# Squared-ReLU attention and a two-layer block on one core: quad 5 turned by a transposing transfer

## The chip, the cores and the metric

The kernel runs on one core of one Trainium2 chip. The metric is the device time of one execution in microseconds (us), the median of three runs. A core has five engines with a queue of instructions each: TensorE (PE in the profile; its weight loads are PEld), VectorE (DVE), ScalarE (ACT), GpSimd (POOL) and SyncE (SP). Transfers run on 16 DMA engines that the queues share.

## The reference

Attention with a squared ReLU in place of softmax, for 8 batch rows, 12 heads, 448 positions and a head size of 64. Its result, as 3584 rows of 768, goes through two matrix products with a PReLU between them.

```python
scores = scale * np.matmul(q, k.transpose(0, 1, 3, 2))      # scale = 1/sqrt(64)
attn = np.maximum(scores, 0.0) ** 2 / S                     # S = 448
attn_out = np.matmul(attn, v)                               # (8, 12, 448, 64)
x = attn_out.transpose(0, 2, 1, 3).reshape(B * S, H * D)    # (3584, 768)
h = x @ w_in                                                # w_in (768, 2048)
g = np.maximum(h, 0.0) + alpha * np.minimum(h, 0.0)
out = g @ w_out                                             # w_out (2048, 768)
```

All inputs and the output are float32.

## The kernel before

The work is written out in the order in which each engine does it. Four heads of one batch row are a *quad*: there are 24, three for each batch row (0 to 2 belong to row 0, 3 to 5 to row 1, 6 to 8 to row 2). For each quad:

- q and k are loaded and cast to bf16 by GpSimd's queue (`load_qk`), v likewise (`load_v`);
- q and k are turned, so that the head size lies on the partitions (the tile `T`). This happens in one of two ways: 28 small transposes on TensorE and two copies out of PSUM (`turn_pe`, quads 0 to 5), or two copies into a tile `perm` on VectorE and one transposing transfer on SyncE's queue (`turn_dma`, quads 6 and later);
- seven chunks of scores go through ReLU (`sc`) and square (`sq`), and the product with v sums over the seven chunks (`attnv`); two copies, half each on ScalarE and VectorE, leave it in `xT`.

For each batch row `f1(b, ff)` makes block `ff` of 16 of the first product and its PReLU, which goes into `gT`; `f2(sb, c, hf)` makes 128 output rows of one half of w_out's columns from all 16 blocks of `gT`, for two batch rows at a time. A burst of attention work for the next rows stands between these long products.

```python
    raw_pool = ctx.enter_context(tc.tile_pool(name="raw", bufs=3))
    v_pool = ctx.enter_context(tc.tile_pool(name="v", bufs=7))
    perm_pool = ctx.enter_context(tc.tile_pool(name="perm", bufs=2))
    T_pool = ctx.enter_context(tc.tile_pool(name="T", bufs=4))
    # ... cut ...
    def hold():                       # the PSUM bank taken longest ago, kept until take() gives it back
        i = min(range(8), key=lambda i: (taken[i], i))
        taken[i] = 10**9
        return i
    # ... cut ...
    def load_w_out(h):
        nc.gpsimd.dma_start(out=w_out_sb[:, h], in_=w_out_v[h])
    # ... cut ...
    def turn_pe(n, parts=(("q", 0, NJ, "D"), ("k", 0, NJ, "D"))):
        if n not in T:
            T[n] = T_pool.tile([128, 2, NJ, 128], BF16, tag="T", name="T")
        for name, lo, hi, eng in parts:
            ps = take_bank().bitcast(BF16)
            for j in range(lo, hi):
                for s in range(2):
                    nc.tensor.transpose(ps[64 * s:64 * s + 64, 128 * j:128 * j + 128], raw[(n, name)][:, s, j], ident)
            dst = T[n][:, "qk".index(name), lo:hi].rearrange("p j c -> p (j c)")
            copy = nc.vector.tensor_copy if eng == "D" else nc.scalar.copy
            copy(dst, ps[:, 128 * lo:128 * hi])

    def turn_dma(n):
        p = perm_pool.tile([128, 2, NJ, 2, D], BF16, tag="perm", name="perm")
        for i, name in enumerate("qk"):
            nc.vector.tensor_copy(p[:, i], raw.pop((n, name)).rearrange("p s j d -> p j s d"))
        t = T_pool.tile([128, 2, NJ, 128], BF16, tag="T", name="T")
        nc.sync.dma_start_transpose(out=t.rearrange("p a j c -> p (a j) c"),
                                    in_=p.rearrange("p a j s d -> p (a j s d)"))
        T[n] = t
    # ... cut ...
    def f1_out(ps, b, ff):            # PReLU of one block, then one waiting square
        neg = neg_pool.tile([128, S], F32, tag="neg", name="neg")
        nc.scalar.activation(neg, ps, ACTF.Relu, scale=-1.0)
        nc.vector.scalar_tensor_tensor(gT[b // 2][:, ff, (b % 2) * S:(b % 2) * S + S],
                                       neg, beta_sb[:, ff:ff + 1], ps, ALU.mult, ALU.add)
        sq(1)
    # ... cut ...
    f1s(0, 10, 12)
    sc(ch(3, 6, 7) + ch(4, 0, 2, "AA"))
    f1s(0, 12, 16)
    f2(0, 0, 0)
    sc(ch(4, 2, 5, "AAADAAA"))
    attnv(3)
    sc(ch(4, 5, 7, "AAAAAAD"))
    turn_pe(5)
    sq(3)
    sq(2, "A")
    load_qk(8)
    load_v(8)
    f2(0, 1, 0)
    sc(ch(5, 0, 3))
    attnv(4)
    sc(ch(5, 3, 5, "AAAADAA"))
    sq(3)
    sq(2, "A")
    f2(0, 2, 0)
    sc(ch(5, 5, 7, "AAAAAAD"))
    sq(1, "A")
    sq(1)
    # ... cut ...
    early = []
    for ff in range(4):
        ps = take_bank()[:, :S]
        f1_mm(ps, 1, ff, range(4))    # four of six matmuls: those of quads 3 and 4
        early.append(ps)
        if ff == 1:
            attnv(5)
    for ff in range(KF):
        if ff < 4:
            f1_mm(early[ff], 1, ff, range(4, KM))
            f1_out(early[ff], 1, ff)
        else:
            f1(1, ff)
        if ff in (1, 4, 7):
            turn_dma(6 + ff // 3)
        if ff == 11:
            load(9)
            load(10)
    f2(0, 3, 0)
    run(some(3))                      # the first scores of quad 6
    f2(0, 3, 1)
    # ... cut ...
```

The letters in `ch(...)` say which engine does the ReLU of a chunk: A for ScalarE, D for VectorE.

Of the kernel before, what the change touches and what calls it, by code (L numbers as in the profile page):

```python
# [11 lines left out]
BF16 = mybir.dt.bfloat16  # L12
# [8 lines left out]
def kernel(  # L21
# [10 lines left out]
    nc = tc.nc  # L32
    B, H, S, D = q.shape
# [3 lines left out]
    KM = d_model // 128  # L37
    KF = d_ff // 128
# [5 lines left out]
    singles = ctx.enter_context(tc.tile_pool(name="singles", bufs=1))  # L44
# [14 lines left out]
    w_out_sb = singles.tile([128, 2, KF, HALF], BF16)  # L59
    alpha_sb = singles.tile([128, KF], F32)  # L60
    beta_sb = singles.tile([128, KF], F32)
    psum = ps_pool.tile([128, 8, 512], F32)


# [3 lines left out]
    def take(lo, n):  # L68
        clock[0] += 1
        for i in range(lo, lo + n):  # L70
            taken[i] = clock[0]

    def take_pair():
        lo = min((0, 2, 4, 6), key=lambda i: (max(taken[i], taken[i + 1]), i))
        take(lo, 2)
        return psum[:, lo:lo + 2]

    def hold():
# [5 lines that stand above are left out]
    def take_bank():  # L84
        i = min(range(8), key=lambda i: (taken[i], i))
        take(i, 1)
        return psum[:, i]
# [4 lines left out]
    def load_qk(n):  # L92
        b, g = divmod(n, NG)
        for name, src in (("q", q), ("k", k)):
            t = raw_pool.tile([128, 2, NJ, D], BF16, tag=name, name=f"{name}raw")
            flat = src[b].rearrange("(m two) (pp j) d -> (two pp) m (j d)", two=2, j=NJ)
            nc.gpsimd.dma_start(out=t.rearrange("p m j d -> p m (j d)"), in_=flat[:, 2 * g:2 * g + 2])  # L97
            raw[(n, name)] = t

    def load_v(n):  # L100
        b, g = divmod(n, NG)
        t = v_pool.tile([128, 2, NJ, D], BF16, tag="v", name="vraw")
        flat = v[b].rearrange("(m two) (pp j) d -> (two pp) m (j d)", two=2, j=NJ)
        nc.gpsimd.dma_start(out=t.rearrange("p m j d -> p m (j d)"), in_=flat[:, 2 * g:2 * g + 2])  # L104
        vraw[n] = t

    w_in_v = moe_w_in.rearrange("(g hf e pp) f -> hf e pp g f", hf=2, e=2, pp=64)
    w_out_v = moe_w_out.rearrange("(kf p) (h c) -> h p kf c", p=128, h=2)
# [5 lines left out]
                nc.gpsimd.dma_start(out=w_in_sb[64 * hf:64 * hf + 64, :, e, lo:hi],  # L114
                                    in_=w_in_v[hf, e, :, :, lo:hi])

    def load_w_out(h):
        nc.gpsimd.dma_start(out=w_out_sb[:, h], in_=w_out_v[h])

    FIRST = 4  # L120
    first, flat0 = {}, {}
    for name, src, eng, hi in (("q", q, nc.sync, NJ), ("k", k, nc.scalar, FIRST)):
# [7 lines left out]
                        in_=flat0["k"][:, :, FIRST * D:])  # L130
# [12 lines left out]
    T = {}  # L143
# [21 lines that stand above are left out]
# [31 lines left out]
    def attnv(n):  # L196
        ps = take_pair()
        vv = vraw.pop(n)
        for j in range(NJ):
            a = att.pop((n, j))  # L200
            for r in range(2):
                for s in range(2):
                    nc.tensor.matmul(ps[64 * s:64 * s + 64, r, :S],  # L203
                                     vv[64 * r:64 * r + 64, s, j, :],
                                     a[64 * r:64 * r + 64, s],
                                     start=(j == 0), stop=(j == NJ - 1))
        b, g = divmod(n, NG)
        if g == 0:
            xT[b] = xT_pool.tile([128, NG, 2, S], BF16, tag="xT", name="xT")
        if n == 0:  # L210
            nc.scalar.activation(xT[b][:, g], ps[:, :, :S], ACTF.Copy, scale=out_scale)
            return
        nc.scalar.activation(xT[b][:, g, 0], ps[:, 0, :S], ACTF.Copy, scale=out_scale)  # L213
        nc.vector.tensor_scalar(xT[b][:, g, 1], ps[:, 1, :S], out_scale, None, ALU.mult)  # L214

    late = []

    def sc(chunks):

        for n, j, eng in chunks:  # L220
            late.append((n, j, relu(score_mm(n, j), eng)))

    def sq(k=99, eng="D"):
        for g in late[:k]:
            square(*g, eng)
        del late[:k]
# [8 lines left out]
    def f1_mm(ps, b, ff, ks):  # L235
        for km in ks:
            nc.tensor.matmul(ps, w_in_sb[:, km // 2, km % 2, bass.ts(ff, 128)],  # L237
                             xT[b][:, km // 2, km % 2, :],
                             start=(km == 0), stop=(km == KM - 1))

    def f1_out(ps, b, ff):
        if b // 2 not in gT:
            gT[b // 2] = g_pool.tile([128, KF, 2 * S], BF16, tag="g", name="gT")
# [5 lines that stand above are left out]
# [6 lines left out]
    def f2(sb, c, hf, parts=((0, HALF),)):  # L255
        o = o_pool.tile([128, HALF], F32, tag="o", name="osb")
        for lo, hi in parts:
            ps = take_bank()[:, :hi - lo]
            for ff in range(KF):
                nc.tensor.matmul(ps, gT[sb][:, ff, bass.ts(c, 128)], w_out_sb[:, hf, ff, lo:hi],  # L260
                                 start=(ff == 0), stop=(ff == KF - 1))
            nc.scalar.copy(o[:, lo:hi], ps)  # L262
            for u in range(2):
                blk = 2 * c + u
                b, j = 2 * sb + blk // NJ, blk % NJ
                rows = out[b * S:(b + 1) * S].rearrange("(pp j) d -> j pp d", j=NJ)
                eng = nc.scalar if u and hi - lo < HALF else nc.sync
                eng.dma_start(out=rows[j][:, hf * HALF + lo:hf * HALF + hi], in_=o[64 * u:64 * u + 64, lo:hi])  # L268
# [4 lines left out]
    def ch(n, lo, hi, p=pat):  # L273
        return [(n, j, p[j]) for j in range(lo, hi)]
# [22 lines left out]
    sq(1)  # L297
    sc([(1, 4, "D"), (1, 5, "A"), (1, 6, "A")])
    sq(2)
    load_w_out(0)  # L300
    load_v(3)
    early = {}
    todo = []
# [8 lines left out]
    sc(ch(2, 0, 3, "AAA"))  # L312
    sq(3)
    attnv(1)
    load_qk(5)
    load_v(4)
    load_v(5)
    load_w_out(1)
    todo = [(ff, km) for ff in range(4) for km in range(4)]
    sc(ch(2, 3, 5, "AAAAAAA"))  # L320
    sq(2)
# [14 lines left out]
    def f1s(b, lo, hi):  # L336
        for ff in range(lo, hi):
            f1(b, ff)
# [9 lines left out]
        load(n + 2)  # L348

    turn_pe(3)  # L350
    load_qk(6)
    load_v(6)
    f1s(0, 4, 6)
    sc(ch(3, 0, 3))
    f1s(0, 6, 8)
# [2 lines left out]
    ps = take_bank()[:, :S]  # L358
    f1_mm(ps, 0, 9, range(KM))
    turn_pe(4, (("q", 0, NJ, "A"), ("k", 0, NJ, "D")))  # L360
    f1_out(ps, 0, 9)
    load_qk(7)
    load_v(7)
    f1s(0, 10, 12)
    sc(ch(3, 6, 7) + ch(4, 0, 2, "AA"))
    f1s(0, 12, 16)
    f2(0, 0, 0)
    sc(ch(4, 2, 5, "AAADAAA"))
    attnv(3)
    sc(ch(4, 5, 7, "AAAAAAD"))  # L370
    turn_pe(5)
    sq(3)
    sq(2, "A")
    load_qk(8)
    load_v(8)
    f2(0, 1, 0)
    sc(ch(5, 0, 3))
    attnv(4)
    sc(ch(5, 3, 5, "AAAADAA"))
    sq(3)  # L380
    sq(2, "A")
    f2(0, 2, 0)
    sc(ch(5, 5, 7, "AAAAAAD"))
    sq(1, "A")
    sq(1)


    chunks = [(n, j) for n in range(2 * NG, NQ) for j in range(NJ)]
# [12 lines left out]
        sq()  # L401

    early = []
    for ff in range(4):
        ps = take_bank()[:, :S]
        f1_mm(ps, 1, ff, range(4))
        early.append(ps)
        if ff == 1:
            attnv(5)
    for ff in range(KF):  # L410
        if ff < 4:
            f1_mm(early[ff], 1, ff, range(4, KM))
            f1_out(early[ff], 1, ff)
        else:
            f1(1, ff)
        if ff in (1, 4, 7):
# [4 lines that stand above are left out]
# [77 lines left out]
```

## Time and profile before

| what | value |
|---|---|
| time, median of 3 runs | 387.88 us (387.86 to 388.0) |
| span of the profiled execution | 386.1 us |
| transposes on TensorE (L152) | 2 x 84, from quads 0 to 5 |
| transposing transfers (T<-perm) | 18 |
| loads by GpSimd's queue (software_dynamic) | 22.45 MB |
| outputs and transposing transfers (mostly hardware_dynamic) | 19.65 MB |

In a row of the profile, a line such as L260 is the line of the kernel, "x16" the number of instructions, and `out<-in` what is written from what. The chain of waits is followed back from the last instruction, at each step to what released it; its pieces are given in order of time as start, length, what. A wait in square brackets is the idle time of an engine before a group and what ended it. The rows with 40 digits or numbers cut the span into 40 slices of 9.65 us: the digits are busy shares in tenths. The lines named most often are L174 (scores), L203 (the product with v), L237 (first product), L260 (second product), L152 (transposes on TensorE), L160 (copies into perm), L162 (the transposing transfer), L246 (gT).

### The profile page before, as it was taken

The numbers are of one execution on the slowest core, as the hardware profiler recorded it, in microseconds if no ns is written. First come the engines' busy times: TensorE is split into PE (matmuls) and PEld (weight loads), VectorE is DVE, ScalarE is ACT, GpSimd is POOL, SyncE is SP. The second block draws the span as 40 slices with busy tenths as digits, with TensorE's granted clock in tenths as the row PEclk, the third lists the DMA queues.
The fourth block names the chain that finished last, engine by engine and source line by source line (L and its number), as shares of the span: only waits on it lengthen the run. The fifth ranks groups of instructions, "written<-read, shape, count | busy, mean of one in ns | idle before, by whom it ended". The sixth has DMA issues, their size and how long they took to land.

```text
span 386.1 us, 7917 instructions
## 1 busy us (share of the span) xinstructions
PE 377.9 (98%) x3228; PEld 211.1 (55%) x3228; DVE 265.8 (69%) x421; ACT 206.2 (53%) x332; POOL 64.0 (17%) x95
## 2 busy tenths in 40 slices
PE   7799999999999999999999999999999999999996
PEld 6444564555665456555555455654555545655564
DVE  4987786776868978789655896689754887626300
ACT  5978696346454664465444654547543475434311
POOL 7567221421012202022100221020000000000000
PEclk9999999999999999999999999999999999999999
DMA  9999999999293765687192871937024300120023
GB/s 160 189 203 204 204 213 220 169 184 213 67 169 51 117 127 86 127 131 120 42 181 51 132 121 42 181 55 134 22 63 109 71 0 23 42 61 2 14 70 82
DMA packets 71365, 42.97 MB, mean 111 GB/s; under 512 B 38432, under 2 KB 71328, under 8 KB 71328
## 3 DMA queue, kind: packets, MB, share of 16 engines
q0 software_dynamic: 26768, 22.45, 39.8%
q1 hardware_dynamic: 44128, 19.65, 23.4%
q8 instruction: 25, 0.41, 0.4%
q10 hardware_dynamic: 432, 0.36, 0.3%
q14 instruction: 12, 0.10, 0.1%
HBM read 45.62 MB, written 11.01 MB: 147 GB/s over the span
## 4 chain that ended last, share of the span: by engine, by line
PE 94%; DVE 3%; DMA 1%; ACT 0%; ACTq 0%; issue 0%
PE psum L237 38%; PE psum L260 38%; PE psum L174 9%; PE psum L203 8%; DVE at L193 2%; DMA qfirst<-in_q_dram 1%; PE psum L152 1%; DVE T L155 1%; DVE rl L185 1%; ACT osb L262 0%; ACTq L268 0%; DVE qraw L136 0%; ACT T L155 0%; ACTq L262 0%
## 5 line engine op out<-in xcount | busy, mean ns | idle before, releaser
L260 PE MATMUL psum<-w_out_sb,gT 128*128 128x384 bf16 (+2 forms) x912 | 151.1, 323 | 0.0
L237 PE MATMUL psum<-xT,w_in_sb 128*128 128x448 bf16 x768 | 149.8, 353 | 0.0
L260 PEld LDWEIGHTS <-gT 128*128 128x128 bf16 x912 | 86.7, 98 | 63.0 <-issue 8.2
L237 PEld LDWEIGHTS <-w_in_sb 128*128 128x128 bf16 x768 | 73.6, 98 | 72.3 <-issue 5.8
L246 DVE SCALAR_TENSOR_TENSOR gT<-neg,beta_sb,psum 128x448 bf16<-128x448 f32 x128 | 83.2, 677 | 29.8 <-ACT neg L245 29.8
L245 ACT ACTIVATE neg<-psum 128x448 f32<-128x448 f32 x128 | 69.2, 546 | 63.3 <-PE psum L237 59.0
L183 ACT ACTIVATE rl<-psum 128x896 bf16<-128x896 f32 x112 | 97.3, 935 | 0.5 <-PE psum L174 0.5
L193 DVE TENSOR_TENSOR at<-rl 128x896 bf16<-128x896 bf16 x162 | 90.6, 616 | 0.0
L185 DVE TENSOR_SCALAR rl<-psum 128x896 bf16<-128x896 f32 x56 | 60.8, 1086 | 43.2 <-PE psum L174 43.2
L262 ACT COPY osb<-psum 128x384 f32<-128x384 f32 (+2 forms) x57 | 27.0, 473 | 105.3 <-PE psum L260 98.5
L174 PE MATMUL psum<-T 64*64 64x448 bf16 x672 | 45.5, 356 | 3.0 <-DVE T L155 1.1
L97 POOL DMA_DIRECT2D qraw<-in_q_dram x23 | 16.6, 720 | 171.0 <-DVE perm L160 161.7
L203 PE MATMUL psum<-at,vraw 64*64 64x448 bf16 x672 | 37.4, 351 | 0.3 <-DVE at L193 0.2
L203 PEld LDWEIGHTS <-vraw 64*64 64x64 bf16 x672 | 24.1, 106 | 10.8 <-issue 2.9
L174 PEld LDWEIGHTS <-T 64*64 64x64 bf16 x672 | 18.2, 106 | 21.5 <-issue 14.4
L214 DVE TENSOR_SCALAR xT<-psum 128x448 bf16<-128x448 f32 x23 | 14.4, 624 | 16.3 <-PE psum L203 11.9
L97 POOL DMA_DIRECT2D kraw<-in_k_dram x23 | 16.6, 722 | 14.8 <-PE psum L237 7.2
L104 POOL DMA_DIRECT2D vraw<-in_v_dram x24 | 17.5, 728 | 1.7 <-DMA qraw<-in_q_dram 0.6
L213 ACT ACTIVATE xT<-psum 128x448 bf16<-128x448 f32 x23 | 12.7, 550 | 3.3 <-PE psum L203 3.3
L160 DVE COPY perm<-qraw 128x896 bf16<-128x896 bf16 x18 | 11.0, 611 | 2.6 <-DMA T<-perm 2.6
L114 POOL DMA_DIRECT2D w_in_sb<-in_moe_w_in_dram x16 | 10.1, 633 | 6.1 <-DMA kraw<-in_k_dram 1.9
L160 DVE COPY perm<-kraw 128x896 bf16<-128x896 bf16 x18 | 10.9, 607 | 0.0
(24 smaller groups left out, 41.6 us busy)
## 6 DMA issues: line engine op xcount, KB each, us to landing
out_dram<-osb SPq DMA_DIRECT2D x110, 96.0 KB, 2.2
vraw<-in_v_dram POOLq DMA_DIRECT2D x24, 224.0 KB, 7.7
qraw<-in_q_dram POOLq DMA_DIRECT2D x23, 224.0 KB, 4.8
kraw<-in_k_dram POOLq DMA_DIRECT2D x23, 224.0 KB, 6.6
w_in_sb<-in_moe_w_in_dram POOLq DMA_DIRECT2D x16, 192.0 KB, 8.3
w_out_sb<-in_moe_w_out_dram POOLq DMA_DIRECT2D x2, 1536.0 KB, 18.5
qfirst<-in_q_dram SPq DMA_DIRECT2D x1, 448.0 KB, 4.1
T<-perm SPq DMA_TRANSPOSE x18, 6.9
```

The lines of the kernel that those rows point to most:

```text
L97: nc.gpsimd.dma_start(out=t.rearrange("p m j d -> p m (j d)"), in_=flat[:, 2 * g:2 * g + 2])
L160: nc.vector.tensor_copy(p[:, i], raw.pop((n, name)).rearrange("p s j d -> p j s d"))
L174: nc.tensor.matmul(ps[64 * c:64 * c + 64, r, :S], t[64 * r:64 * r + 64, 1, j, 64 * c:64 * c + 64], t[64 * r:64 * r + 64, 0, :, 64 * c:64 * ...
L183: nc.scalar.activation(rl, ps[:, :, :S], ACTF.Relu)
L185: nc.vector.tensor_scalar(rl, ps[:, :, :S], 0.0, None, ALU.max)
L193: nc.vector.tensor_tensor(a, rl, rl, ALU.mult)
L203: nc.tensor.matmul(ps[64 * s:64 * s + 64, r, :S], vv[64 * r:64 * r + 64, s, j, :], a[64 * r:64 * r + 64, s], start=(j == 0), stop=(j == NJ ...
L237: nc.tensor.matmul(ps, w_in_sb[:, km // 2, km % 2, bass.ts(ff, 128)], xT[b][:, km // 2, km % 2, :], start=(km == 0), stop=(km == KM - 1))
L245: nc.scalar.activation(neg, ps, ACTF.Relu, scale=-1.0)
L246: nc.vector.scalar_tensor_tensor(gT[b // 2][:, ff, (b % 2) * S:(b % 2) * S + S], neg, beta_sb[:, ff:ff + 1], ps, ALU.mult, ALU.add)
L260: nc.tensor.matmul(ps, gT[sb][:, ff, bass.ts(c, 128)], w_out_sb[:, hf, ff, lo:hi], start=(ff == 0), stop=(ff == KF - 1))
L262: nc.scalar.copy(o[:, lo:hi], ps)
```

## The change

Quad 5 is turned by a transposing transfer instead of on TensorE, so that 28 transposes leave TensorE's queue. For the transfer to have the DMA engines nearly to itself, other loads make room: quad 5's q and k are loaded ahead of w_out's first half (which now comes in four pieces), and w_out's second half and all loads of quads 6 to 8 are held back by one tiny copy on GpSimd that reads the transfer's result. To give the transfer time, quad 5's scores are moved behind one more `f2`, its last two chunks behind two early blocks of the next product, and `attnv(5)` behind four; a fifth early block is added behind it. The early blocks now hold their PSUM banks. In quad 5 two squares go from ScalarE to VectorE and one ReLU, that of the last chunk, from VectorE to ScalarE; one waiting square of quad 4 is put behind the copies into perm.

```diff
+    landed = singles.tile([1, 1], BF16)
...
-    def load_w_out(h):
-        nc.gpsimd.dma_start(out=w_out_sb[:, h], in_=w_out_v[h])
+    def load_w_out(h, step=KF):
+        for lo in range(0, KF, step):
+            nc.gpsimd.dma_start(out=w_out_sb[:, h, lo:lo + step], in_=w_out_v[h][:, lo:lo + step])
...
-    load_w_out(0)
+    load_qk(5)
+    load_w_out(0, 4)
     load_v(3)
...
     attnv(1)
-    load_qk(5)
     load_v(4)
     load_v(5)
-    load_w_out(1)
...
     turn_pe(3)
-    load_qk(6)
-    load_v(6)
...
-    load_qk(7)
-    load_v(7)
     f1s(0, 10, 12)
     sc(ch(3, 6, 7) + ch(4, 0, 2, "AA"))
-    f1s(0, 12, 16)
+    f1s(0, 12, 14)
+    kept = late[:]
+    del late[:]
+    f1s(0, 14, 16)
+    turn_dma(5)
+    late += kept
+    nc.gpsimd.tensor_copy(landed, T[5][:1, 0, 0, :1])
+    load_qk(6)
+    load_qk(7)
+    load_qk(8)
+    load_v(6)
+    load_v(7)
+    load_v(8)
+    load_w_out(1)
     f2(0, 0, 0)
+    sq()
     sc(ch(4, 2, 5, "AAADAAA"))
     attnv(3)
     sc(ch(4, 5, 7, "AAAAAAD"))
-    turn_pe(5)
     sq(3)
     sq(2, "A")
-    load_qk(8)
-    load_v(8)
+    sq()
     f2(0, 1, 0)
+    f2(0, 2, 0)
     sc(ch(5, 0, 3))
+    sq(1)
     attnv(4)
     sc(ch(5, 3, 5, "AAAADAA"))
-    sq(3)
-    sq(2, "A")
-    f2(0, 2, 0)
-    sc(ch(5, 5, 7, "AAAAAAD"))
-    sq(1, "A")
-    sq(1)
+    sq()
...
-    for ff in range(4):
-        ps = take_bank()[:, :S]
-        f1_mm(ps, 1, ff, range(4))
-        early.append(ps)
+    for ff in range(5):
+        early.append(hold())
+        f1_mm(psum[:, early[ff], :S], 1, ff, range(4))
         if ff == 1:
+            sc(ch(5, 5, 7))
+            sq(1)
+            sq(1, "A")
+        if ff == 3:
             attnv(5)
     for ff in range(KF):
-        if ff < 4:
-            f1_mm(early[ff], 1, ff, range(4, KM))
-            f1_out(early[ff], 1, ff)
+        if ff < 5:
+            f1_mm(psum[:, early[ff], :S], 1, ff, range(4, KM))
+            f1_out(psum[:, early[ff], :S], 1, ff)
+            take(early[ff], 1)
         else:
             f1(1, ff)
```

## The prediction

> **What bounds the kernel now.** I read the busy shares, then the chain of waits, then the chain piece by piece between 40 and 90 us, because the change touches only the stretch from about 28 to 80 us. On the page:
>
> ```profile
> PE 377.9 (98%) x3228; PEld 211.1 (55%) x3228; DVE 265.8 (69%) x421; ACT 206.2 (53%) x332; POOL 64.0 (17%) x95
> PE 94%; DVE 3%; DMA 1%; ACT 0%; ACTq 0%; issue 0%
> ```
>
> TensorE is busy 98% of the span and is 94% of the chain that ended last. What is not TensorE lies before 20 us, which the change leaves alone. So only two things move the time: matmul instructions taken out of TensorE's stream, and gaps put into it. The chain in order of time shows the piece that goes, and its surroundings without a gap:
>
> ```profile
> 45.29 2.60 PE psum L260 x16
> 47.89 0.69 PE psum L174 x12
> 48.58 1.39 PE psum L203 x28
> 49.98 0.38 PE psum L174 x8
> 50.35 0.90 PE psum L152 x28
> 51.26 2.71 PE psum L260 x16
> ...
> 59.64 1.62 PE psum L237 x8
> 61.26 1.45 PE psum L203 x28
> 62.70 16.75 PE psum L237 x88
> 79.46 2.60 PE psum L260 x16
> ```
>
> The 28 instructions at 50.35 us are turn_pe(5): 0.90 us. The next quads (6, 7, 8) already go through transposing transfers, so the question is what such a transfer costs those who wait for it. VectorE's timeline in the following stage has the only wait of that kind:
>
> ```profile
> 70.39 1.85 DVE L246 SCALAR_TENSOR_TENSOR gT<-neg,beta_sb,psum 128x448 bf16<-128x448 f32 x3
> 74.80 0.62 DVE L160 COPY perm<-qraw 128x896 bf16<-128x896 bf16 x1 [2.55 <-DMA T<-perm]
> 75.33 0.61 DVE L160 COPY perm<-kraw 128x896 bf16<-128x896 bf16 x1
> 75.86 4.90 DVE L246 SCALAR_TENSOR_TENSOR gT<-neg,beta_sb,psum 128x448 bf16<-128x448 f32 x8
> ```
>
> Quad 8's copy into perm needs the buffer that quad 6's transfer reads (perm has two), so VectorE stands 2.55 us, and eight gT results queue up behind. They end at 75.86 + 4.90 = 80.76 us. f2(0,3,0), at 79.46 in the chain, reads gT of the second batch row block by block: its 16th matmul comes about 15 x 0.17 = 2.5 us (2.71 / 16 each) after its start, near 81.9. So this wait is hidden by about 1.1 us only. I keep that number.
>
> The transfers, from the view of one tile's transfers and from the page's issue table:
>
> ```profile
> DMA to landing us min/median/max: 3.4/6.9/12.6
> w_out_sb<-in_moe_w_out_dram POOLq DMA_DIRECT2D x2, 1536.0 KB, 18.5
> DMA  9999999999293765687192871937024300120023
> GB/s 160 189 203 204 204 213 220 169 184 213 67 169 51 117 127 86 127 131 120 42 181 51 132 121 42 181 55 134 22 63 109 71 0 23 42 61 2 14 70 82
> ```
>
> The first is T, the transposed rows: 3.4 us at best, 12.6 at worst. The last two say that the DMA engines are full until about 96 us, at some 200 GB/s. Landing times in narrow windows are 7.0 us for quad 6 (issued at 67.72), 11.1 for quad 7 and 12.6 for quad 8, issued with more loads in flight.
>
> **What the Trainium skill says.** "DMA: Bandwidth & Descriptors", section "DMA Transpose (X-bar)": the plain DMA transpose is issued from the Sync or Scalar queue and takes 2-byte types. It fits the trace: the loads with a cast from f32 are on POOL's queue, the transposes on SP's, and the copy into perm on VectorE (0.61 us for q, 0.61 for k) stays part of the price. The same page, "Queues, rings and completion order": each DMA engine goes round robin between the queue rows that have work, a packet at a time. By that a transfer on SP's queue isn't put behind a backlog on POOL's, but shares with it; the spread from 3.4 to 12.6 us agrees. "TensorE: Matmul & The Clock Gate", "Back-to-back issue gap", gives about 81 ns for a matmul of 128 columns with its weight load. Here 0.90 / 28 = 32 ns, so the measurement decides, and the gain is smaller than the page would give.
>
> **The change, part by part.**
> (a) Removed: turn_pe(5), 28 transposes, 0.90 us of TensorE on the chain, and its two copies out of PSUM (VectorE, about 1.1 us for the pair), which were off it. No other TensorE instruction is added or lost. Gain 0.90.
> (b) Quad 5's transfer. In VectorE's timeline gT's last operation of the first batch row starts at 46.81 us; one square of 0.54 before it is now put behind, so it starts near 46.3 and ends near 46.9. Two copies into perm (1.1 us) end near 48.0: the transfer is issued there. It is needed by sc(5,0). After the change TensorE goes from 50.35 through two f2 of 2.7 us, so that is at 55.75. It may take 7.7 us.
> (c) What is in its way: POOL's queue up to v of quad 5. In narrow windows w_out's first half landed at 43.9 (29.42 + 14.5), v3 at 45.0, and the following 224 KB loads about 1.15 us apart. With quad 5's q and k (448 KB, 2.3 us) put ahead, the last quarter of w_out's half lands near 46.2, v3 near 47.3, v5 near 49.5. w_out's last quarter is needed by the 13th matmul of f2(0,0,0), at 45.1 + 12 x 0.17 = 47.2, v3 at attnv(3) at 48.6: both hold by about 1 us. The transfer then meets 1.5 us of rest and no other load, as POOL waits for it: an estimate of 4 to 6 us, landing between 52 and 54. Holds by 2 to 4 us.
> (d) The bursts of quad 5. Scores (5,0..2) at 55.75, attnv(4), two more at 57.85, two after the second early group, near 59.7, attnv(5) near 61.6. The slowest road is ScalarE: relu of (5,5), relu of (5,6), 0.93 each by the row of line 183, then the square of (5,6), 0.97 by the row of line 191: from 59.95 to 62.75. attnv(5) needs that square for its last of seven steps, at about 61.6 + 6 x 0.2 = 62.8. It just holds; I charge 0.1 us. After attnv(5) only one early group (0.75 us) covers xT, against two before: xT's VectorE half ended 0.77 us after attnv in the kernel before (62.85 + 0.62 against 62.70), and its first reader comes second after the group, 0.94 after. Holds.
> (e) The loads held back: quads 6 to 8 are 9 x 224 KB and w_out's half 1536 KB, in all 3.64 MB, with four output transfers of 96 KB. At 0.213 MB per us (the sixth slice of the GB/s row) that is 19 us from about 53: until 72. Quad 6 lands near 57 and its copy comes at 66; w_out's half is needed by f2(0,3,1) near 82. Both hold.
> (f) But (e) puts about 1 MB (4.8 us) in flight when quad 6's transfer is issued, which is near 67.4 now (0.3 earlier, since the fifth early group moves matmuls ahead of it). In the kernel before, the tail of one load (landed at 69.1) and quad 9's loads, 672 KB, met it: not much less. If it takes L, perm(8) and eight gT operations end at 67.4 + L + 1.1 + 4.9. TensorE is 0.9 to 1.1 us earlier here: f2(0,3,0) starts near 78.4 and its last gT is read at 80.9. There is no wait while L is under about 7.4; it was 7.0. Each us beyond costs a us. With L about 7.5 on average and some spread, I charge 0.3 us.
>
> Sum: 387.88 - 0.90 + 0.1 + 0.3 = 387.4; since each wait is more likely absent than there, I put the middle at 387.3.
>
> **The rivals.**
> 1. The wait moves to quad 6's transfer (f). For it: 1.1 us of cover before, of which the gain itself eats nearly all, and landing times of 11.1 and 12.6 us for transfers issued into fuller queues. Against: sharing by packets, and a backlog much like that of before. With L of 9 to 10 it makes 388.5 to 389.5. I give it 3 in 10 to cost over 0.9 us and so turn the gain into nothing or a loss.
> 2. Quad 5's transfer itself lands after 55.75. For: 7 us was the median landing, 7.7 us is the allowance. Against: those ran among loads, this one nearly alone, and the fastest, late in the kernel where the DMA engines are little used, took 3.4. 1 in 10; then 387.5 to 390, and quads 6 to 8 would be later too, so rival 1 comes with it.
> 3. Nothing waits, and the whole 0.90 is kept: 387.0 or a little under. 4 in 10.
> 4. w_out's first half or v3 late by (c): under 1 us, 1 in 8.
> VectorE can't become the bound as a whole: it has 69%, and what it gets and loses is nearly even: two copies into perm of 0.61 us for two out of PSUM of 0.6, two squares of 0.62 for a ReLU of 1.09.
>
> **Range and chances.** Low end 386.6: the full 0.90 and a little for joints (the chain's 0.90 hides fill at its two ends). High end 389.2: rival 1 with L near 9.5. 2% is 7.8 us; no single part comes near it on either side, 1 in 100 each.
>
> **What would show it.** L152 loses 28 of its 168 instructions, and the chain goes from L174 at about 50 us straight to two L260 groups of 16. T has 19 transfers; the first is issued near 48 and lands before 54. VectorE's wait for T before perm is near 2.5 to 4 us at about 72 to 76. If rival 1 holds, the chain shows VectorE's gT ahead of L260 near 80 us. If rival 2, TensorE's L174 near 56 waits for the transfer. I'm wrong if the time falls under 386.6, which would need a gain that this chain doesn't show, or if a gap of over 2 us opens in TensorE between 45 and 90 us.

## The result, and the profile after

| | before | after |
|---|---|---|
| time, median of 6 runs each | 387.94 us | 396.25 us |
| ratio, with its 95% interval | | 1.0218 (1.0203 to 1.0233) |
| span of the profiled execution | 386.1 us | 394.0 us |
| transposing transfers | 18 | 19 |
| end of f2(0,3,0) in the chain | 82.06 us | 89.65 us |

The kernel became 2.2% slower, 8.3 us, where 0.6 us less was predicted. The page of the changed kernel has the busy row, the shares of the chain by engine, and TensorE's granted clock in 40 slices of 9.85 us:

```profile
PE 379.3 (96%) x3200; PEld 211.5 (54%) x3200; DVE 265.7 (67%) x422; ACT 205.3 (52%) x331; POOL 66.4 (17%) x99
PE 90%; DMA 5%; DVE 3%; issue 0%; ACT 0%; ACTq 0%; DVEq 0%
PEclk9999999969999999999999999999999999999999
```

A transfer has come into the chain, and in one slice, from 79 to 89 us, the clock is down. The chain of waits piece by piece says which transfer (start, length, what):

```profile
50.73 5.31 PE psum L262 x32
...
62.23 1.45 PE psum L205 x28
63.68 4.24 PE psum L239 x22
67.92 15.34 DMA T<-perm
...
83.38 1.15 DVE perm L162 x2
84.53 0.60 DVE gT L248
85.12 0.04 issue
85.17 4.48 PE psum L262 x16
```

It is not the new transfer. Two f2 follow each other at 50.73 without a gap, and quad 5's work runs on through attnv(5) at 62.23. What stands there is quad 6's transfer, issued at 67.92 and landed at 83.26. VectorE's timeline shows how it reaches TensorE:

```profile
70.61 1.85 DVE L248 SCALAR_TENSOR_TENSOR gT<-neg,beta_sb,psum 128x448 bf16<-128x448 f32 x3
83.38 0.62 DVE L162 COPY perm<-qraw 128x896 bf16<-128x896 bf16 x1 [10.93 <-DMA T<-perm]
84.45 4.81 DVE L248 SCALAR_TENSOR_TENSOR gT<-neg,beta_sb,psum 128x448 bf16<-128x448 f32 x8
```

The wait before quad 8's copy was 2.55 us before and is 10.93 now. All eight PSUM banks hold blocks that VectorE hasn't read, so TensorE, done with the first product at 78.92, can't start f2(0,3,0) until the first of them is out, at 85.17.

The bill can be read off the two chains. TensorE ran 0.38 us late from the start (22.18 against 21.80 at the same piece; this varies from run to run). It saved 0.92 up to the end of the first product: 78.92 against 79.46. It then stood 6.25 us, and the 16 matmuls of f2(0,3,0) took 4.48 us instead of 2.60. 0.38 - 0.92 + 6.25 + 1.88 = 7.59, the 7.59 between the two ends of f2(0,3,0). The remaining 0.3 of the profiled 7.9 us is after the last matmul.

The 1.88 us look like the clock that TensorE was granted. In the view of busy time by windows (window, us, busy of PE, PEld, DVE, ACT, POOL, then clock, DMA share, GB/s):

```profile
81.00:82.00 1.00, 0.00 (x0) 0.00 (x0) 0.00 (x0) 0.00 (x0) 0.00 (x0) 0.77 1.23 193
...
85.00:86.00 1.00, 0.83 (x3) 0.40 (x3) 1.00 (x3) 0.74 (x2) 0.52 (x1) 0.50 1.24 194
88.00:89.00 1.00, 1.00 (x6) 0.57 (x5) 1.00 (x3) 0.12 (x1) 0.00 (x0) 0.81 1.36 228
89.00:90.00 1.00, 1.00 (x16) 0.36 (x13) 0.26 (x1) 0.31 (x1) 0.00 (x0) 1.00 1.31 253
```

The clock fell to half in the gap, near 81.5, and came back about 3.2 us after TensorE had work again. But VectorE's last gT result, which the 16th matmul reads, came only at 84.45 + 4.81 = 89.26 us, and at full clock f2(0,3,0) could not have ended before about 89.26 + 0.17 = 89.4. So the clock cost some 0.2 us here; the rest of the 1.88 is the pace of VectorE, 0.6 us a block, and belongs to the late transfer.

### The profile page after: what moved, and what is told of

Read it like the earlier page. It is cut to its first block, busy times and chain, and to the rows that moved or that the text cites. A ratio compares the mean times of both kernels' runs of the same rounds, so it can differ in the third digit from the quotient of the medians.

```text
span 394.0 us, 7870 instructions
## 1 busy us (share of the span) xinstructions
PE 379.3 (96%) x3200; PEld 211.5 (54%) x3200; DVE 265.7 (67%) x422; ACT 205.3 (52%) x331; POOL 66.4 (17%) x99
## 4 chain that ended last, share of the span: by engine, by line
PE 90%; DMA 5%; DVE 3%; issue 0%; ACT 0%; ACTq 0%; DVEq 0%
PE psum L262 38%; PE psum L239 35%; PE psum L176 9%; PE psum L205 8%; DMA T<-perm 4%; DVE at L195 2%; DMA qfirst<-in_q_dram 1%; PE psum L154 1%; DVE T L157 1%; DVE rl L187 1%; DVE perm L162 0%; ACT osb L264 0%; DVE gT L248 0%; ACTq L270 0%; DVE qraw L138 0%
## 5 line engine op out<-in xcount | busy, mean ns | idle before, releaser
L262 PE MATMUL psum<-w_out_sb,gT 128*128 128x384 bf16 (+2 forms) x912 | 152.7, 326 | 6.3 <-DVE gT L248 6.3
L195 DVE TENSOR_TENSOR at<-rl 128x896 bf16<-128x896 bf16 x164 | 91.7, 616 | 0.0
L187 DVE TENSOR_SCALAR rl<-psum 128x896 bf16<-128x896 f32 x55 | 59.7, 1086 | 43.7 <-PE psum L176 43.7
L176 PEld LDWEIGHTS <-T 64*64 64x64 bf16 x672 | 18.2, 105 | 21.5 <-issue 14.8
L215 ACT ACTIVATE xT<-psum 128x448 bf16<-128x448 f32 x23 | 12.6, 550 | 2.5 <-PE psum L205 2.5
## 6 DMA issues: line engine op xcount, KB each, us to landing
w_out_sb<-in_moe_w_out_dram POOLq DMA_DIRECT2D x4, 384.0 KB, 10.5
```

What stands on the lines that cost most here:

```text
L176: nc.tensor.matmul(ps[64 * c:64 * c + 64, r, :S], t[64 * r:64 * r + 64, 1, j, 64 * c:64 * c + 64], t[64 * r:64 * r + 64, 0, :, 64 * c:64 * ...
L187: nc.vector.tensor_scalar(rl, ps[:, :, :S], 0.0, None, ALU.max)
L195: nc.vector.tensor_tensor(a, rl, rl, ALU.mult)
```

## Why quad 6's transfer was late: theory and rivals

Theory A: the transfer shares the DMA engines with the loads on GpSimd's queue *packet for packet*, not byte for byte. The DMA view from 72 to 82 us of the changed kernel, and from 72 to 73 of the kernel before (queue, kind: packets, MB, share of 16 engines):

```profile
q0 software_dynamic: 1670, 1.34, 90.3%
q1 hardware_dynamic: 1673, 0.43, 39.2%
```

```profile
q1 hardware_dynamic: 1132, 0.29, 127.3%
```

After its issue at 67.92 no packet of the transfer moved until about 71.9. From there on, in ten us, the two queues moved the same number of packets, but a load's packet has 802 bytes (1.34 MB / 1670) and a transposing one 257. So the transfer, 448 KB or 1792 packets, got a quarter of the bytes and needs 1792 / 167 = 10.7 us of sharing. The kernel before moved 1132 of these packets in a single us, because just then GpSimd's queue moved none: its view has no line for q0. Quad 8's last load had landed at 69.1, and four loads of quads 9 and 10, issued from 68.1 on, had yet to land (the first of them at 74.7). Why they stood still isn't shown; turns by packets alone don't explain it. The windows of that kernel (columns as above) show the lull:

```profile
66.00:68.00 2.00, 2.00 (x13) 1.03 (x11) 2.00 (x4) 1.17 (x3) 0.58 (x1) 1.00 1.18 192
68.00:72.00 4.00, 4.00 (x23) 2.08 (x22) 4.00 (x8) 2.08 (x4) 3.33 (x6) 1.00 0.92 109
72.00:76.00 4.00, 4.00 (x23) 2.07 (x22) 1.45 (x4) 1.18 (x3) 0.40 (x1) 1.00 1.28 226
```

This is behind the 7.0 us of the kernel before, and it was luck of timing, not sharing.

The rivals: (B) the loads of quads 9 and 10 delay it, not w_out; (C) the gap comes from the new order or the held banks, not from perm; (E) one more transposing transfer delays the others, whatever is in flight; (F) the one large w_out transfer as such stops it; (H) the cause lies with quad 5's new way at all.

## The experiments

All of them are compared with the kernel before, run on the same chip. The first five ask for the cause, the others for a version that keeps the gain.

**The cause put into the kernel before** (d1_before_extra_load). Quad 5 stays on TensorE; w_out's second half is loaded once more than needed.

```diff
     load_qk(8)
     load_v(8)
+    load_w_out(1)
```

> The kernel before, with one thing added: w_out's second half is loaded a second time, behind the loads of quad 8. Nothing computed changes, and quad 5 is turned on TensorE. Theory A: that load (1.57 MB, issued near 60) is still in the queue when quad 6's transfer is issued at 67.7, so the transfer goes packet for packet with it and with quads 9 and 10, lands after 13 to 15 us instead of 7, and the kernel before becomes slower by about as much as the changed one: 393 to 396 us. Rival H (what slows the changed kernel is in its new order of work or in quad 5's transfer): the extra load is hidden, 388 us.

Measured: 395.40 us, ratio 1.0190 (1.0175 to 1.0206); quad 6's transfer took 15.1 us. VectorE's and TensorE's timelines:

```profile
83.16 0.62 DVE L160 COPY perm<-qraw 128x896 bf16<-128x896 bf16 x1 [10.74 <-DMA T<-perm]
```

```profile
84.95 3.99 PE L260 MATMUL psum<-w_out_sb,gT 128*128 128x384 bf16 x15 [5.32 <-DVE gT L246]
```

The same two waits at the same places, with nothing of the change in it but a load in flight. H, E and C are not needed for this gap: it takes neither quad 5's transfer nor the new order.

**A third perm buffer** (e1_perm3).

```diff
-    perm_pool = ctx.enter_context(tc.tile_pool(name="perm", bufs=2))
+    perm_pool = ctx.enter_context(tc.tile_pool(name="perm", bufs=3))
```

> The changed kernel with three perm buffers instead of two. Theory A (quad 6's transfer is slow because it shares the DMA engines packet for packet with loads, and costs time only through the perm buffer that VectorE waits for): the transfer still takes about 15 us and lands near 83.3, but quad 8's copy doesn't wait, gT is ready, and TensorE waits only at the first scores of quad 6, needed at 81.6: a gap of about 1.7 us, no loss of clock, about 389.0 us. Rival C (TensorE's wait has to do with the new order or the banks held, not with perm): the gap before f2(0,3,0) stays, over 394 us.

Measured: 396.78 us, 1.0236 (1.0203 to 1.0270). The first half of the expectation held: the transfer took 15.5 us, the gap before f2(0,3,0) went, and TensorE stood 2.00 us at quad 6's scores. The sum of 389.0 did not hold. TensorE's gaps, ScalarE's wait, and SyncE's queue:

```profile
83.44 0.76 PE L176 MATMUL psum<-T 64*64 64x448 bf16 x12 [2.00 <-DMA T<-perm]
...
105.16 1.40 PE L176 MATMUL psum<-T 64*64 64x448 bf16 x12 [3.78 <-ACT rl L185]
```

```profile
103.81 0.48 ACT L264 COPY osb<-psum 128x384 f32<-128x384 f32 x1 [7.08 <-DMA out_dram<-osb]
```

```profile
67.85 25.65 SPq L164 DMA_TRANSPOSE T<-perm  x3
93.60 3.88 SPq L270 DMA_DIRECT2D out_dram<-osb  x6
```

With perm free, transfers 7 and 8 are issued sooner into the same full DMA engines. SyncE's queue is occupied with the three of them until 93.5 us, and the output transfers stand behind in that queue. The four osb buffers run out, ScalarE waits 7.08 us to write the next, its ReLUs come late, and TensorE stands 3.78 us. The clock dropped to half after either gap (the 32 matmuls behind the first took 6.99 us instead of 5.31). So perm was only the first of two places where a slow transfer reaches TensorE; to free it moves the wait. The slow transfer itself has to go.

**Loads of quads 9 and 10 held back** (e2_hold910): behind quad 6's transfer, with w_out still beside it.

```diff
             turn_dma(6 + ff // 3)
+            if ff == 1:
+                nc.gpsimd.tensor_copy(landed, T[6][:1, 0, 0, :1])
```

> The changed kernel with the loads of quads 9 and 10 held back until quad 6's transfer has landed; w_out's second half is still in flight beside it. Theory A: at the transfer's first packet (near 71.9) some 0.7 MB of w_out are left, 900 packets of 768 bytes; they go one for one with the transfer's 256-byte packets at 180 a us, 5 us, and its other 900 alone in 1 us: landing near 79, 11 us after issue. f2(0,3,0) then ends some 4 us late: 391 to 392 us. Rival B (the loads of quads 9 and 10 are what delays it): it lands in 7 us, and the time is near 387.3. Rival D (the size of the load doesn't matter, any backlog does): still 15 us, 396 us.

Measured: 392.15 us, 1.0112 (1.0089 to 1.0135). In the profiled execution, at 393.8 us the slowest of four, the transfer took 12.7 us and the gap before f2(0,3,0) was 3.66. This is nearer to A's 11 us, and 391 to 392 us, than to B's 7 or D's 15: w_out and the later loads each have their part, as packets in flight.

**w_out's second half behind quad 6's transfer** (e3_wout_behind6), with the loads of quads 9 and 10 behind it in the queue.

```diff
     load_v(8)
-    load_w_out(1)
...
             turn_dma(6 + ff // 3)
+            if ff == 1:
+                nc.gpsimd.tensor_copy(landed, T[6][:1, 0, 0, :1])
+                load_w_out(1, 4)
```

> The changed kernel with w_out's second half, in four pieces, held back until quad 6's transfer has landed, and with it the loads of quads 9 and 10 that stand behind it in the queue. Theory A: the queue is empty when the transfer is issued, it lands in 4 to 5 us (near 72), no wait before f2(0,3,0). w_out's last piece then lands near 81 to 84 and is needed near 84.3; quad 9's rows come late for their copy near 85: 0 to 1.5 us. About 387.3 to 388.5 us. Rival E (one more transposing transfer delays the others whatever else is in flight): quad 6's transfer stays over 10 us, over 392 us.

Measured: 394.93 us, 1.0175 (1.0155 to 1.0195). The transfer landed in 4.1 us; the DMA view from 68 to 71 us shows it alone:

```profile
q1 hardware_dynamic: 1808, 0.46, 78.9%
```

E falls: it is one more transfer, and quad 6's is the fastest of all these runs. But my estimate for w_out was wrong by the same mistake read backwards. Quad 8's transfer now shares with w_out, packet for packet, and slows it: the pieces took 7.0, 9.0, 11.0 and 13.2 us, and quad 8's transfer 15.3. TensorE's timeline:

```profile
84.72 0.81 PE L262 MATMUL psum<-w_out_sb,gT 128*128 128x384 bf16 x4 [1.48 <-DMA w_out_sb<-in_moe_w_out_dram]
87.61 6.19 PE L262 MATMUL psum<-w_out_sb,gT 128*128 128x384 bf16 x20 [2.09 <-DMA w_out_sb<-in_moe_w_out_dram]
```

**All loads where they were before** (e4_loads_as_before), quad 5's transfer and the new order kept.

```diff
-    load_qk(5)
-    load_w_out(0, 4)
+    load_w_out(0)
     load_v(3)
...
     attnv(1)
+    load_qk(5)
     load_v(4)
     load_v(5)
+    load_w_out(1)
... (loads of quads 6 to 8 back in their places, the copy into landed taken out)
```

> The changed kernel's order of work with quad 5's transfer, but all loads where they were in the kernel before. Theory A: w_out's second half and quads 6 and 7 are in flight when quad 5's transfer is issued near 48.5: about 3.5 us to the first packet and 1792 packets at 180 a us make 13 to 14 us, landing near 62 where 55.9 is needed: a gap of 6 us, with the lower clock after it 1.8 more, about 395 us; quad 6's transfer then meets an emptier queue and is not late. Rival E (transfers cost the same whatever is in flight): quad 5's takes 4 us as in the changed kernel, and the time is under 388 us.

Measured: 397.41 us, 1.0259 (1.0211 to 1.0306). In the profiled execution, at 401.01 us the slowest of four, quad 5's transfer took 14.8 us instead of 4.1. The DMA view from 53 to 63 us, and TensorE:

```profile
q0 software_dynamic: 1789, 1.44, 89.6%
q1 hardware_dynamic: 1787, 0.52, 35.9%
```

```profile
63.21 1.33 PE L176 MATMUL psum<-T 64*64 64x448 bf16 x12 [7.57 <-DMA T<-perm]
```

One packet for one packet again. So the holding back of loads does for quad 5's transfer what it is meant for; without it the change loses at quad 5 what with it it loses at quad 6. Quad 6's transfer, which I expected to be undisturbed then, met loads of its own and took 10.4 us; TensorE stood another 2.4 us before and in f2(0,3,0).

**Fewer packets beside quad 6's transfer** (b1_gate6, b2_gate7). v of quads 6 to 8 and all loads of quads 9 and 10 stand behind quad 6's transfer, or behind quad 7's; q and k of quads 6 to 8 and w_out's second half stay where the change put them.

```diff
     load_qk(8)
-    load_v(6)
-    load_v(7)
-    load_v(8)
     load_w_out(1)
...
             turn_dma(6 + ff // 3)
+            if ff == 1:                       # b2: ff == 4 and T[7]
+                nc.gpsimd.tensor_copy(landed, T[6][:1, 0, 0, :1])
...
-            load(9)
+            load_qk(9)
+            load_v(6)
+            load_v(7)
+            load_v(8)
+            load_v(9)
             load(10)
```

> The changed kernel, but v of quads 6 to 8 and all loads of quads 9 and 10 stand behind quad 6's transfer; q and k of quads 6 to 8 and w_out's second half stay ahead of it. Theory A: the queue held 3.64 MB when quad 5's transfer landed, now 2.95; 2.15 of it had moved by 67.9 in the changed kernel, so the rest of 0.8 MB is through at about 72, when the transfer's first packets run. They run alone: landing near 74.5, no gap before f2(0,3,0), 387.0 to 387.6 us. Quad 8's transfer shares with the held loads, lands near 90, and is needed near 99. Rival F (it is w_out's transfer as such, one of 1536 KB, that stops the transposing one): landing after 78 as in the run with quads 9 and 10 held, 391 us.

> As the run before it, but the held loads stand behind quad 7's transfer instead of quad 6's. Theory A: transfers 6, 7 and 8 all run almost alone (4 to 7 us each), quad 9's rows land near 83, before their copy at 85: 387.0 to 387.4 us. Rival G (the held loads then come too late for quad 9): VectorE waits before perm near 85, and TensorE up to 2 us: 388 to 390 us.

Measured: 390.18 us, 1.0056 (1.0043 to 1.0068), and 389.21 us, 1.0035 (1.0023 to 1.0048). Quad 6's transfer took 8.9 and 9.1 us, not the 6.5 expected: w_out was through near 72 as expected, but for the next 1.5 us or so the DMA engines moved 47 to 223 GB/s, not the 290 of the lull, and later, for 1.4 us (75.3 to 76.7 in b1, 74.6 to 76.1 in b2), next to nothing, 51 GB/s at most. I can't say why. 8.9 us lies between A's 6.5 and F's 10 or more, so it doesn't decide on F; e3 does: beside w_out in four pieces quad 8's transfer still took 15.3 us, 1495 packets against 1523 of the loads from 78 to 86 us. TensorE waited in four steps of 0.25 us inside f2(0,3,0), which took 4.48 us in TensorE's timeline instead of 2.76. Behind quad 6's transfer the outputs were also late again (0.80 us of TensorE near 109, after ScalarE's wait for osb); behind quad 7's that was gone, so the later gate is the better one, and G's wait for quad 9 didn't show.

**The same with a quarter of w_out ahead of quad 5's transfer** (b3_gate7_quarter), and **with three perm buffers** (b4_gate7_perm3, the edit of e1 on b2).

(`load_w_out(h, step, frm, to)` loads blocks `frm` to `to` of half `h` in pieces of `step`.)

```diff
     load_v(4)
     load_v(5)
+    load_w_out(1, 4, 0, 4)        # blocks 0 to 3; blocks 4 to 15 stay behind quad 5's transfer
```

> As the run before it, with the first quarter of w_out's second half (384 KB, 1.9 us) put ahead of quad 5's transfer, which landed 3.3 us before it was needed. Theory A: quad 5's transfer lands near 54.5, still before 55.9, and quad 6's meets an empty queue: landing within 5 us, 387.0 to 387.3 us. If quad 5's transfer shares with that quarter for longer than thought, TensorE waits at the scores of quad 5 and the time is above 388.

> The version that holds loads behind quad 7's transfer, with three perm buffers. Theory A: the wait for perm is gone, but it was hidden by then, so the time is the same as with two, 387.0 to 387.4. If a wait for perm is still on the path in the version with two buffers, this one is faster by it.

Measured: 387.93 us, 0.9998 (0.9988 to 1.0007), and 388.48 us, 1.0007 (0.9998 to 1.0015). In the first, quad 5's transfer took 5.0 us and held, quad 6's took 7.7, and TensorE's timeline has one step left:

```profile
81.72 0.34 PE L262 MATMUL psum<-w_out_sb,gT 128*128 128x384 bf16 x1 [0.26 <-DVE gT L248]
```

f2(0,3,0) took 3.25 us in that timeline, 0.5 more than 2.76. So 7.7 us of transfer cost 0.5, 8.9 and 9.1 cost 1.7, and 6.3 (c2 below) cost nothing: the prediction's 7.4 us of cover is right to about 0.2. The second, against 389.21 with two buffers, shows that the wait for perm was still on the path there; but its trace has the outputs late by 0.69 us instead.

**w_out's second half in two and in three parts** (c2_two_parts, c1_three_parts): the last quarter behind quad 7's transfer and ahead of quad 9's rows; c1 has the first quarter ahead of quad 5's transfer besides. The other loads are held as in b2.

```diff
     load_v(5)
+    load_w_out(1, 4, 0, 4)        # c1 only
...
     load_qk(8)
-    load_w_out(1)
+    load_w_out(1, 8, 4, 12)       # c2: blocks 0 to 11
...
+            load_w_out(1, 4, 12)  # behind quad 7's transfer
             load_qk(9)
```

> w_out's second half in three parts: a quarter ahead of quad 5's transfer, two quarters behind it, the last quarter behind quad 7's, ahead of quad 9's rows and the other held loads. Theory A: 2.16 MB stand between quad 5's and quad 6's transfer instead of 2.56, through near 68 to 69; quad 6's lands in 4 to 6 us, under the 7.4 that are hidden, so no wait before f2(0,3,0), and the full 0.9 us of the transposes is kept: 387.0 to 387.3 us. If w_out's last quarter is late (needed near 84), TensorE waits in f2(0,3,1): 388 to 389.

> As the three parts, but three quarters behind quad 5's transfer and none ahead of it. 2.56 MB then stand between the two transfers, starting about 1 us earlier than with a quarter ahead. Theory A: quad 6's transfer lands in 6 to 8 us, at the edge of what is hidden: 387.1 to 387.9 us.

Measured: c1 387.79 us, 0.9993 (0.9986 to 0.9999); c2 388.49 us, 1.0010 (1.0003 to 1.0016). In c1 quad 6's transfer took 4.3 us and quad 5's 5.5, and the chain has no gap:

```profile
63.42 15.24 PE psum L239 x80
78.66 2.60 PE psum L262 x16
81.26 0.69 PE psum L176 x12
```

f2(0,3,0) starts at 78.66 where it was 79.46: the transposes' 0.9 us, less 0.12 of a later start. Of this 0.8 the profiled span, of the fastest of 21 runs, keeps 0.6 (385.5 against 386.1) and the median only 0.26, not the 0.9 expected; runs of this kernel spread from 387.31 to 388.46. Its interval is the only one here that lies below 1, by 0.0001, one of eleven: a weak sign of a gain. In c2 quad 6's took 6.3 us, all hidden, but the outputs were late again, by a wait of ScalarE for osb near 105 (2.56 us).

## Why the prediction was wrong, point by point

- (a) was right: TensorE reached the end of the first product 0.92 us earlier, net of its start, against 0.90.
- (b) to (d) were right. Quad 5's transfer was issued at 48.46 and landed at 52.6 (48.0, and 52 to 54); w_out's last quarter landed at 46.5 (46.2), v3 at 47.8 (47.3). The bursts of quad 5 run without a gap. Rival 2 and rival 4 did not happen.
- (e): the loads were meant to be through at 72. q, k and v of quads 6 to 8 were; w_out's half landed at 79.4. Some 0.6 to 0.7 MB of it were still to come at 72, just when the transfer took its first turns: of the 3.64 MB, only 0.16 had moved from 54 to 56. The rest then went at the pace of the turns.
- (f) is the step that failed, and rival 1 the way it went. The place, the perm buffer, the 7.4 us of cover and "each us beyond costs a us" were right: with 15.3 us the excess is 7.9, and TensorE lost 6.25 + 1.88 = 8.1. What was wrong is one term, L: 7.5 us assumed, 9 to 10 allowed under rival 1, 15.3 measured; the high end of 389.2 rested on 9.5. Three things made it too small. I took the 7.0 us of the kernel before as a transfer among loads, "not much less", although it had run in a lull: 109 GB/s from 68 to 72 us, about half of what the stretches beside it show. The page's slice from 67.55 to 77.20, with its 169 GB/s, averages this away, and I read it as full. I put 1 MB in flight at the transfer's issue; of the 3.64 MB of (e) some 2.15 had moved by then, so it was 1.5. And I took "shares" for halves of the bytes. "DMA: Bandwidth & Descriptors" of the Trainium skill, section "Queues, rings and completion order", says that an engine drains a whole packet of one queue before it turns to the next; its packet is a group of typically 9 to 17 descriptors, and whether the profile counts the same thing isn't shown here. The packets that the profile counts go one for one to within 1% (1670 against 1673), so the counts agree with turns; with 802 bytes against 257 that is a quarter of the bytes, and 10.7 us of sharing besides the wait for the first packet. The landing times of 11.1 and 12.6 us for quads 7 and 8 were transfers of that kind, and I set them aside.
- Of rival 1 I saw one road only, through perm and gT. With that closed, e1 shows a second road to TensorE, through SyncE's queue and the osb buffers.

What stays open: what keeps the first packets of a transfer back (quad 6's waited about 1.2 us from issue in e3, which had no loads in flight, but also in c1 and c2, which had some; 2.1 in b3, 3 to 4 in the others where it was followed), why the loads stood still in the lull of the kernel before, and the slow tail in b1 and b2.

## What to carry to other kernels

A transfer's duration here belonged to what was in flight beside it, 4.1 us or 15.3 for the same 448 KB: before moving one, look at the packets and their sizes in the stretch where it will run, and for one measured elsewhere, ask whether it ran in a lull. Two queues that take turns by packets give the one with small packets the smaller share, a quarter here, so these transposing transfers needed a window without loads, and a load that was held back to make one window filled the next. When a step is freed by another buffer, follow the slow thing to the next place where it is waited for.

## What the runs showed of the hardware that was not expected

- Transposing packets of some 257 bytes went at about 180 a us beside loads and at 800 to 1130 a us alone in the fastest stretches (after, e3, before); a transfer of 448 KB took 4.1 us alone and 14.8 to 15.5 beside loads.
- The clock was halved after a gap shorter than I had thought. "TensorE: Matmul & The Clock Gate" of the Trainium skill, section "Why this matters for your kernels", advises no gaps over about 3 us. In e1 a gap of 2.00 us, from 81.44 to 83.44, was followed by half clock from about 84.7 to 88, which cost some 1.7 us on 32 matmuls, nearly as much again as the gap. Gaps of 0.80 us (b1) and 1.33 us (e4) left it at full.
- Issuing a transposing transfer occupied SyncE's queue far longer beside loads: in e1 the three took 5.3, 10.5 and 9.6 us of it without a break, in c1 1.8, 2.7 and 1.5.
